# Batch 2's second DFT-47 step ahead of the first tokens, with banks copied into buffers of the turned rows

## The chip, the cores and the metric

The kernel runs on one core of a Trainium2 chip. The metric is the device time of one execution in microseconds (us). The chip's TensorE (PE) multiplies matrices from SBUF into PSUM banks; ScalarE (ACT) and VectorE (DVE) copy, cast and combine; SyncE (SP) and GpSimd (POOL) issue transfers (DMAs) between SBUF and DRAM. The engines run side by side and wait for each other through semaphores.

## The reference

For each of 8 batches of 3008 x 256 values: a real FFT along the sequence, a complex 256 x 256 product with bias, a soft threshold, the inverse FFT; then a feed-forward layer on all 24064 tokens.

```python
X = np.fft.rfft(x, axis=1)
Yr = Xr @ w_r - Xi @ w_i + b_r
Yi = Xr @ w_i + Xi @ w_r + b_i
Yr = np.sign(Yr) * np.maximum(np.abs(Yr) - lam, 0.0)   # Yi likewise
y = np.fft.irfft(Y, n=x.shape[1], axis=1)
h = y.reshape(B * S, D) @ w_in
out = (h * (1.0 / (1.0 + np.exp(-1.702 * h)))) @ w_out
```

## The kernel before, in words

3008 is 64 x 47, so the FFT is done as DFT-47 and DFT-64 products. For each batch, eight DFT-47 steps (`dft47`, L495) take 48 x 512 pieces of x, fill two PSUM banks by four products, copy the banks to SBUF (`dft47_out`, L507, on ACT here) and store them in a DRAM buffer `s1`, one per batch. Later stages (`spectral`, L515) read `s1`, mix, invert, and store to `s2`, from which the tokens come. Each 512 tokens then run through the feed-forward layer in eight parts (`Ffn.up`, `Ffn.down`).

Batch 0 has its own start-up (`first_batch`, L369) in a pool `su` of SBUF, with no trip through `s1`. In it, `rows` (three buffers of 2 KB per partition) hold the turned rows of the first DFT, and `xp` (five pairs, L478) hold pieces of x. Beside batch 0's stages, PE does batch 1's eight DFT-47 steps (`early(n)`, L867) and then one of batch 2 (`do_early(0)`, L938). Their evictions go to `buf2` (L139), seven buffers of one tag that many tiles share.

The change lies where batch 0 ends. Its last inverse step (`stage_inv(5)`) is evicted and stored to `s2`, once by POOL and once by SP (L469). The last third of the first two token pieces can be loaded only then (`load_first`, L605, on SP). While PE waits for it, it runs ten unread products `wm` (L941). Then the pool `su` closes (L948), the pool `ff` opens on the same SBUF, and the first tokens are made (`first_tokens`, L615): products in a bank, a cast to `th` on ACT, the rest `tl` on DVE (`split`, L148). With these the first `Ffn.up` (L694) begins. During the first eight parts, the other steps of batch 2 (`do_early(n)`, n from 1 to 7) and the rounding of further weights (`weights`) run beside it.

Each engine runs its instructions in order. The order on each is set by a scheduler that simulates the program when it is built; `after(...)` holds an instruction behind a named one. SP's transfers take eight completion semaphores (DMAHW0 to DMAHW7) in turn, so each waits for the one eight before it; POOL's use DMASW0 to DMASW7. A tile that takes over SBUF of an earlier one waits until that one's readers are done.

Of the kernel before, what the change touches and what calls it, by code (L numbers as in the profile page):

```python
# [9 lines left out]
F32 = mybir.dt.float32  # L10
# [10 lines left out]
D, DFF = 256, 2048  # L21
# [95 lines left out]
def fourier_mix_then_gated_ffn(ctx: ExitStack, tc: tile.TileContext, x, w_r, w_i, b_r, b_i, w_in, w_out, pack, kbs, out):  # L117
    nc = tc.nc
# [8 lines left out]
    ps_o = ctx.enter_context(tc.tile_pool(name="ps_o", bufs=1, space=PSUM))  # L127
    ps_a = ctx.enter_context(tc.tile_pool(name="ps_a", bufs=4, space=PSUM))
    held = ExitStack()
    su = held.enter_context(tc.tile_pool(name="su", bufs=1))  # L130
    ff = None

    def bank():
        return ps_a.tile([128, 512], F32, name="pa", tag="pa")

    def buf(shape, dt, name, tag=None, bufs=2):
        return wk.tile(shape, dt, name=name, tag=tag or name, bufs=bufs)

    def buf2(name):  # L139
        return buf([128, 2, D], F32, name, tag="w2", bufs=W2)  # L140

    def after(*keys):
        held = ExitStack()
        for k in keys:
            held.enter_context(tc.issue_after(done_at[k]))
        return held
# [5 lines left out]
    last = [None]  # L152

    def mm(ps, w, t, start=True, stop=True):
        last[0] = nc.tensor.matmul(ps, lhsT=w, rhs=t, start=start, stop=stop).ins  # L155
# [9 lines left out]
    def const(shape, dt, name):  # L165
        return cst.tile(shape, dt, name=name, tag=name.rstrip("_"))
# [10 lines left out]
    parts, done_at = {}, {}  # L177
# [41 lines left out]
    def packs_in():  # L219
        pk = ff.tile([128, PKR], F32, name="pk", tag="gt", bufs=1)  # L220
        nc.sync.dma_start(pk, packs)
        return pk

    def rounded_parts(pk):
        parts["i"] = const([128, 2, 2, 128], F32R, "ki_")
        parts["f"] = const([128, NS], F32, "fg_")
        nc.scalar.copy(parts["i"].rearrange("p h z n -> p (h z n)"), pk[:, 0:512])
        nc.scalar.copy(parts["f"], pk[:, 512:536])
        wr, wi = buf2("wr"), buf2("wi")
        for t, w in ((wr, w_r), (wi, w_i)):  # L230
            nc.sync.dma_start(t, w.rearrange("(c p) e -> p c e", p=128))
        parts["h"] = const([128, 3, 2, D], F32R, "wf_h")
        parts["l"] = const([128, 3, 2, D], F32R, "wf_")
        split(parts["h"][:, 2], parts["l"][:, 2], wr)
        for i, op in ((0, ALU.add), (1, ALU.subtract)):
            t = buf2("wd")
            nc.vector.scalar_tensor_tensor(t, wr, -1.0, wi, ALU.mult, op)
            split(parts["h"][:, i], parts["l"][:, i], t)
# [4 lines left out]
    room = [cst.tile([128, NQ // 2 * 896], F32, name=f"room{i}", tag=f"wo_{i}") for i in range(2)]  # L243
# [78 lines left out]
    def weights(n):  # L322
        (down_weights if n % 2 else up_weights)(n // 2)
        if n >= 9:
            load_weights(n + 3)
        elif n in (4, 5):
            load_weights(n + 2)
# [25 lines left out]
    def quarters():  # L353
        return tc.manual_schedule(engines={mybir.EngineType.PE})
# [123 lines left out]
    def xpair():  # L478
        return su.tile([128, 1024], F32, name="xp", tag="xp", bufs=5)

    def xload(b, n, *ts):

        w = 1024 // len(ts)
        for k, t in enumerate(ts):
            for p in range(2):
                at = 1024 * n + w * k
                nc.sync.dma_start(t[64 * p:64 * p + 48], x[b].rearrange("(n p) c -> p n c", p=2)[p, :, at:at + w])
        return [t[:, at:at + 512] for t in ts for at in range(0, w, 512)]
# [3 lines left out]
    def new_s1(b):  # L492
        s1s[b] = dr.tile([2, 64, 2, 8, 2, D], F32, name="s1")

    def dft47(b, n, t, first=None, other=None):  # L495

        ps = [bank(), bank() if other is None else other]
        with quarters():
            if first:
                first(ps[0])  # L500
            dft47_products(ps, t)
        dft47_out(b, n, ps)

    def dft47_products(ps, t):
        for c, p in ((1, 1), (0, 0), (0, 1), (1, 0)):
            mm(ps[p][64 * c:64 * c + 64], kp[64 * p:64 * p + 48], t[c][64 * p:64 * p + 48])

    def dft47_out(b, n, ps, first=nc.scalar.copy):
        s1w = s1s[b].rearrange("c f p n j d -> (c f) p n (j d)")
        for p in range(2):  # L510
            ev = buf2("aev").rearrange("p j d -> p (j d)")
            (nc.scalar.copy if p else first)(ev, ps[p])  # L512
            nc.sync.dma_start(s1w[:, p, n], ev)

    def spectral(b, s2):  # L515
        s1r, s2w = dram_views(s1s[b], s2)
# [83 lines left out]
    def load_first(u, r0, r1, queue):  # L600

        if u not in us:
            us[u] = buf([128, 4, D], F32, "ur", tag="sx", bufs=3) if u else const([128, 4, D], F32, "wf_h")
        s2w = s2s[0].rearrange("c p j d -> (c p) j d")
        done_at["u"] = queue.dma_start(us[u][r0:r1], s2w[r0:r1, 4 * u:4 * u + 4]).ins  # L605
# [32 lines left out]
    def tokens(u):  # L638
# [20 lines left out]
        if step:  # L659
            dft47_out(b, n, p47, nc.vector.tensor_copy)  # L660
# [163 lines left out]
    def new_s2(b):  # L824
        s2s[b] = dr.tile([48, 2, NJ, D], F32, name="s2")
        return s2s[b]
# [3 lines left out]
    def tokens_to(n):  # L830
        nonlocal done
        while done < NB * NU and JP * done < n:
            load_u(done)
            load_x(done)
            if done < 2:
                load_u(done + 1)
            tokens(done)
            done += 1
        load_u(done)
        load_x(done)  # L840
# [22 lines left out]
    x1 = []  # L863
    EARLY = 4
    BLOCKS = (0, 1, 2, 4, 5, 7, 8, 10)

    def early(n):  # L867
        with after(("m", 3 + 2 * n) if n < EARLY else ("m", 11) if n == EARLY else ("i", 5)):
            dft47(1, n, x1[n], claim_now if n < EARLY else None)
        done_at["x", n] = last[0]  # L870

    for n in range(14):
# [29 lines left out]
        if n == 11:  # L902
            early(3)
# [9 lines left out]
        if n == 12:  # L913
            with after(("m", 11), ("t", 11), ("s", 11)):
                i0(4)
                early(EARLY)
# [2 lines left out]
                i0(5)  # L919
    for u in range(2):  # L920
        load_first(u, 64, 96, nc.sync)
    for n in range(EARLY + 1, 8):
        with after("u", ("e", 5)):
            early(n)
    xr = {}

    def load_early(n):
        if n < 8:
            ts = [buf2("xr") if n % 2 else buf([128, 2, D], F32, "xr", tag="co") for c in range(2)]
            xr[n] = xload(2, n, *(t.rearrange("p j d -> p (j d)") for t in ts))  # L930

    def do_early(n):
        load_early(n + 1)
        dft47(2, n, xr.pop(n), claim, ps_o.tile([128, 512], F32, name="po3", tag="po3"))

    load_early(0)
    with after(("x", 7), "u"):
        do_early(0)  # L938
    done_at["x", 8] = last[0]
    for n in range(2):  # L940
        wm = ps_o.tile([128, 512], F32, name="wm", tag=f"po{n}")  # L941
        for i in range(5):
            with after(("x", 8)):
                mm(wm, wi_h[:, 0, 0:128], wi_h[:, 0, 0:512])
    with after(("e", 5), ("v", 11)):
        weights(8)
# [7 lines left out]
    queue, nextb, behind = [], 1, None  # L954
    for n in range(NT * NQ):
        k, q = divmod(n, NQ)
        if q == 0:
            cur = Ffn(k)
        if n != 2:
            with after("down") if q == 1 and k > 1 else ExitStack():  # L960
                cur.up(q)
        if n < NQ:
            if n < 7:
                with after("h", "l"):
                    weights(9 + n)
            if n == 1:
                cur.up(2)
            if n:
                do_early(n)
            if n == 6:  # L970
                with after("h", "l"):
                    rounded_parts(pk)
                ahead = spectral(1, new_s2(1))
                ahead.pop(0)[1]()
            if n == 3:
                pk = packs_in()
        elif not queue and nextb < NB and (nextb < 3 or done >= NU * (nextb - 1)):
            queue = ahead if nextb == 1 else spectral(nextb, new_s2(nextb))
            total, spent, n0 = sum(c for c, _ in queue), 0.0, n
            n1 = NQ * S * nextb // TOK - 16  # L980
            nextb += 1
        while queue and spent < total * (n + 1 - n0) / (n1 - n0):
            c, step = queue.pop(0)
            spent += c
            step()
        need = TOK * (1 + (n + 2) / NQ)
        while queue and need + JP > S * (nextb - 1):
            queue.pop(0)[1]()
        if JP * done < need:
            tokens_to(need)  # L990
        if behind is not None:
            with after("up") if q == 1 and k > 1 else ExitStack():
                behind[0].down(behind[1])
        behind = (cur, q)
# [36 lines left out]
```

## Time and profile before

| | us |
|---|---|
| median of 3 runs (2543.94 to 2545.46) | 2544.39 |
| the profiled execution | 2546.47 |
| its span | 2544.7 |
| PE busy in the span | 2523.1 |
| DVE busy | 1959.7 |
| ACT busy | 1609.9 |
| POOL busy | 90.8 |

The profiled execution is one of its own; its span begins with the first instruction, and 1.8 us lie around it. Busy times are those of single engines, which run side by side. PE's granted clock reads 1.00 over nearly all of the span.

### The profile page before, as it was taken

How to read it: one execution, taken by the hardware profiler on the slowest of the kernel's cores; microseconds unless marked ns; L12 is line 12 of the kernel's file. 1: busy time of each engine (PE TensorE's matmuls, PEld its weight loads, DVE VectorE, ACT ScalarE, POOL GpSimd, SP SyncE). 2: the span in 40 equal slices, each digit the busy share in tenths (PEclk: the TensorE clock that was granted, in tenths of full speed). 3: DMA queues.
4: the chain of work that ended last, by engine and by line, in shares of the span. 5: the costliest groups of instructions: out<-in, count | busy, mean ns of one | idle time of the engine just before them, and what ended most of it. 6: DMA issues, size and time to landing. Idle time of an engine off the chain costs nothing.

```text
span 2544.7 us, 49144 instructions
## 1 busy us (share of the span) xinstructions
PE 2523.1 (99%) x19425; PEld 2231.3 (88%) x19425; DVE 1959.7 (77%) x3285; ACT 1609.9 (63%) x2632; POOL 90.8 (4%) x109
## 2 busy tenths in 40 slices
PE   9999999999999999999999999999999999999999
PEld 7779988888898888888888888988889999888888
DVE  6788877777777777777777877778777787777776
ACT  5566666666666666666666666666666666665655
POOL 0000000000000000000000000000000000000000
PEclk9999999999999999999999999999999999999999
DMA  7753332333323323233233233233332232200000
GB/s 215 241 156 89 92 87 84 96 92 96 91 75 98 94 90 96 66 99 104 81 92 90 84 106 88 82 92 95 90 103 57 58 87 58 60 30 22 24 10 17
DMA packets 163749, 221.80 MB, mean 87 GB/s; under 512 B 18288, under 2 KB 120912, under 8 KB 163520
## 3 DMA queue, kind: packets, MB, share of 16 engines
q1 hardware_dynamic: 161904, 212.96, 29.0%
q0 software_dynamic: 1616, 5.70, 0.8%
q8 instruction: 154, 2.52, 0.4%
q14 instruction: 75, 0.61, 0.1%
HBM read 117.40 MB, written 101.19 MB: 86 GB/s over the span
## 4 chain that ended last, share of the span: by engine, by line
PE 92%; DVE 2%; ACT 2%; issue 2%; DMA 1%; SPq 0%; POOL 0%; POOLq 0%; DVEq 0%; ACTq 0%
PE pa L155 57%; PE po L155 35%; DMA room<-in_x 1%; ACT gb L703 0%; ACT ht L149 0%; PE pi L155 0%; DVE gt L736 0%; DVE hb L150 0%; ACT aev L512 0%; DVE lt L709 0%; DVE lt L150 0%; DMA s<-iev 0%; PE pt L404 0%; DVE tl L150 0%; DVE gt L738 0%
## 5 line engine op out<-in xcount | busy, mean ns | idle before, releaser
L703 ACT ACTIVATE gb<-pa 128x512 f32<-128x512 f32 x752 | 446.0, 599 | 363.4 <-PE pa L155 359.1
L150 DVE TENSOR_TENSOR lt<-gt,ht 128x1024 fp32r<-128x1024 f32 x367 | 449.3, 1224 | 238.0 <-ACT ht L149 237.1
L155 PE MATMUL pa<-th,wi_h 128*128 128x512 f32 x1504 | 594.7, 396 | 2.2 <-ACT aev L512 1.7
L155 PE MATMUL pa<-tl,wi_h 128*128 128x512 f32 x1504 | 589.5, 392 | 0.0
L155 PE MATMUL pa<-th,wi_l 128*128 128x512 f32 x1504 | 587.9, 391 | 0.0
L149 ACT CAST ht<-gt 128x1024 fp32r<-128x1024 f32 x367 | 384.8, 1048 | 209.0 <-DVE gt L738 205.6
L736 DVE TENSOR_TENSOR gt<-gb 128x512 f32<-128x512 f32 x367 | 255.8, 697 | 167.4 <-ACT gb L703 159.6
L150 DVE TENSOR_TENSOR hb<-gb,hb 128x768 fp32r<-128x768 f32 x367 | 349.8, 953 | 14.6 <-ACT hb L149 14.4
L155 PEld LDWEIGHTS pa<-th,wi_l 128*128 128x128 f32 x1504 | 282.7, 188 | 58.9
L155 PEld LDWEIGHTS pa<-th,wi_h 128*128 128x128 f32 x1504 | 283.4, 188 | 51.6 <-ACT aev L512 2.7
L155 PEld LDWEIGHTS pa<-tl,wi_h 128*128 128x128 f32 x1504 | 283.4, 188 | 42.4
L149 ACT CAST hb<-gb 128x768 fp32r<-128x768 f32 x367 | 307.3, 837 | 9.7 <-PE po L155 0.5
L155 PE MATMUL po<-hb,wo_0a 128*128 128x256 f32 (+1 forms) x924 | 231.2, 307 | 1.8 <-ACT o L809 1.2
L155 PE MATMUL po<-hb,wo_0b 128*128 128x256 f32 x924 | 230.3, 306 | 0.0
L155 PE MATMUL pa<-wf_h,zz 128*128 128x256 f32 x1008 | 199.5, 282 | 0.0
L155 PE MATMUL po<-ht,wo_0a 128*128 128x256 f32 (+1 forms) x752 | 191.9, 287 | 1.1 <-DVE o L819 0.9
L155 PE MATMUL po<-ht,wo_0b 128*128 128x256 f32 (+1 forms) x752 | 190.7, 287 | 2.2 <-ACT ht L149 2.0
L155 PE MATMUL po<-ht,wo_1a 128*128 128x256 f32 (+1 forms) x752 | 191.9, 285 | 0.0
L155 PE MATMUL po<-ht,wo_1b 128*128 128x256 f32 (+1 forms) x752 | 190.4, 285 | 0.0
L155 PEld LDWEIGHTS po<-hb,wo_0a 128*128 128x128 f32 x924 | 161.4, 189 | 15.0 <-ACT o L809 1.7
L155 PEld LDWEIGHTS po<-hb,wo_0b 128*128 128x128 f32 x924 | 161.0, 189 | 14.2 <-DVE hb L727 0.2
L737 DVE TENSOR_TENSOR gt<-gb,gt 128x256 f32<-128x256 f32 x367 | 161.2, 439 | 6.6
(179 smaller groups left out, 4227.2 us busy)
## 6 DMA issues: line engine op xcount, KB each, us to landing
s<-aev SPq DMA_DIRECT2D x112, 256.0 KB, 3.7
s<-iev SPq DMA_DIRECT2D x95, 256.0 KB, 2.4
ur<-s SPq DMA_DIRECT2D x124, 192.0 KB, 3.6
out<-o SPq DMA_DIRECT2D x93, 256.0 KB, 2.2
br<-s SPq DMA_DIRECT2D x168, 128.0 KB, 2.9
yd<-mv SPq DMA_DIRECT2D x168, 128.0 KB, 2.4
yr<-yd SPq DMA_DIRECT2D x84, 256.0 KB, 3.1
xt<-in_x SPq DMA_DIRECT2D x80, 192.0 KB, 3.6
```

Source lines behind the costliest of these rows:

```text
L149: nc.scalar.copy(hi, src)
L150: return nc.vector.tensor_tensor(lo, src, hi.bitcast(F32), ALU.subtract)
L155: last[0] = nc.tensor.matmul(ps, lhsT=w, rhs=t, start=start, stop=stop).ins
L703: done_at["g"] = nc.scalar.activation(o, ps.rearrange("p (h n) -> p h n", h=2), AF.Gelu_apprx_sigmoid).ins
L736: nc.vector.tensor_tensor(gt[:, 0:2], b12, gb[:, 0:3:2], ALU.subtract)
L737: nc.vector.tensor_tensor(gt[:, 2], gb[:, 2], gt[:, 0], ALU.subtract)
```

## The change

Step 1 of batch 2 is done ahead of the first tokens, behind step 0; its x goes to a pair of `xp`, loaded earlier. Six unread products are left of ten. The banks of the last two steps of batch 1 and one of batch 2's step 0 are copied to `spare`: three `rows` buffers and two halves of another `xp` pair, in place of `buf2`. The stores of batch 2's two steps are issued on POOL in place of SP. Loads of batch 2's pieces are issued one step sooner in the text.

```diff
-    def dft47_out(b, n, ps, first=nc.scalar.copy):
+    def dft47_out(b, n, ps, first=nc.scalar.copy, room=None, queue=nc.sync):
         s1w = s1s[b].rearrange("c f p n j d -> (c f) p n (j d)")
         for p in range(2):
-            ev = buf2("aev").rearrange("p j d -> p (j d)")
+            ev = room.pop(0) if room else buf2("aev").rearrange("p j d -> p (j d)")
             (nc.scalar.copy if p else first)(ev, ps[p])
-            nc.sync.dma_start(s1w[:, p, n], ev)
+            queue.dma_start(s1w[:, p, n], ev)
...
+    def load_early(n, *ts):
+        if n < 8:
+            ts = ts or [buf2("xr") if n % 2 else buf([128, 2, D], F32, "xr", tag="co") for c in range(2)]
...
-    def do_early(n):
-        load_early(n + 1)
-        dft47(2, n, xr.pop(n), claim, ps_o.tile([128, 512], F32, name="po3", tag="po3"))
+    def do_early(n, po=3, **to):
+        if n:
+            load_early(n + 1)
+        dft47(2, n, xr.pop(n), claim, ps_o.tile([128, 512], F32, name=f"po{po}", tag=f"po{po}"), **to)
+
+    load_early(0)
+    load_early(1, xpair())
+    spare = [su.tile([128, 512], F32, name="rows", tag="rows", bufs=3) for n in range(3)]
+    t = xpair()
+    spare += [t[:, 0:512], t[:, 512:1024]]
     for n in range(EARLY + 1, 8):
         with after("u", ("e", 5)):
-            early(n)
...
-    load_early(0)
+            early(n, room=spare if n > EARLY + 1 else None)
     with after(("x", 7), "u"):
-        do_early(0)
+        do_early(0, room=spare, queue=nc.gpsimd)
     done_at["x", 8] = last[0]
+    with after(("x", 8)):
+        do_early(1, 2, queue=nc.gpsimd)
+    done_at["x", 9] = last[0]
     for n in range(2):
         wm = ps_o.tile([128, 512], F32, name="wm", tag=f"po{n}")
-        for i in range(5):
-            with after(("x", 8)):
+        for i in range(3):
+            with after(("x", 9)):
                 mm(wm, wi_h[:, 0, 0:128], wi_h[:, 0, 0:512])
...
-            if n:
+            if n > 1:
                 do_early(n)
```

What this does to the order shows at three places.

ACT, from the evictions of batch 1's last step to the first casts of the tokens, before (aev: a `buf2` buffer; pa, po: banks; what stands in brackets are the semaphores waited for):

```order
L512 COPY aev_1025<-pa_1016 128x512 [waits DVE_49,PE_49]
L512 COPY aev_1028<-pa_1017 128x512 [waits DMAHW6_49,Activation_49]
L512 COPY aev_1053<-pa_1044 128x512 [waits PE_sequencer_49,DMAHW2_49,PE_49,Activation_49]
L512 COPY aev_1056<-po3_1043 128x512 [waits DMAHW3_49,Activation_49]
L149 CAST th_1097<-pa_1092 128x376 [waits PE_49]
L149 CAST th_1097<-pa_1101 128x376 [waits PE_49]
L149 CAST th_1097<-pa_1111 128x136 [waits PE_49]
```

The same place in the changed kernel, from the eviction of step 6's first bank:

```order
L512 COPY rows_995<-pa_1014 128x512 [waits PE_49]
L512 COPY rows_996<-pa_1015 128x512
L512 COPY xp_998<-pa_1028 128x512 [waits PE_49]
L512 COPY rows_997<-pa_1027 128x512 [waits PE_49]
L512 COPY aev_1052<-po3_1040 128x512 [waits DMAHW6_49,PE_49,Activation_49]
L512 COPY xp_998<-pa_1041 128x512 [waits PE_sequencer_49,PE_49]
L512 COPY aev_1071<-pa_1062 128x512 [waits PE_sequencer_49,DMAHW7_49,PE_49,Activation_49]
L512 COPY aev_1074<-po2_1061 128x512 [waits DVE_49]
L149 CAST th_1111<-pa_1106 128x376 [waits DMAHW2_49,DMAHW6_49,PE_49,Activation_49]
L149 CAST th_1111<-pa_1115 128x376 [waits PE_49]
```

Five evictions go to rows and xp buffers and wait for no transfer; of the same five before, four waited for one (two of them ahead of the rows shown); two more evictions stand ahead of the casts; and the first cast, which waited for PE alone, now waits for two transfers of SP, on DMAHW2 and DMAHW6.

SP's queue from the last store of batch 0 to batch 1's last stores, before (s1_101 is batch 1's `s1`; a store that waits for a DMAHW semaphore takes that one itself):

```order
L469 DMA s2_96<-iev_981 128x2x256 [waits DMAHW6_49,Activation_49]
L605 DMA wf_h_905<-s2_96 32x1024 [waits DMAHW6_49,DMAHW3_49,DMAHW7_49,DMAHW2_49,DMASW7_49]
L605 DMA ur_907<-s2_96 32x1024 [waits DMAHW0_49,DMASW1_49]
L513 DMA s1_101<-aev_995 128x512 [waits DMAHW1_49,Activation_49]
L513 DMA s1_101<-aev_998 128x512 [waits Activation_49]
L513 DMA s1_101<-aev_1010 128x512 [waits Activation_49]
L513 DMA s1_101<-aev_1013 128x512 [waits DMAHW4_49,Activation_49]
L613 DMA ur_1108<-s2_96 48x1024 [waits DMAHW5_49]
L487 DMA xr_1037<-in_x 48x512 [waits DVE_49]
L513 DMA s1_101<-aev_1025 128x512 [waits DMAHW7_49,Activation_49]
L513 DMA s1_101<-aev_1028 128x512 [waits DMAHW0_49,Activation_49]
```

The changed kernel, from the first of the loads L605:

```order
L605 DMA wf_h_905<-s2_96 32x1024 [waits DMAHW4_49,DMAHW1_49,DMAHW5_49,DMAHW0_49,DMASW7_49]
L605 DMA ur_907<-s2_96 32x1024 [waits DMAHW2_49,DMASW1_49]
L513 DMA s1_101<-aev_1008 128x512 [waits DMAHW3_49,Activation_49]
L513 DMA s1_101<-aev_1011 128x512 [waits Activation_49]
L513 DMA s1_101<-rows_995 128x512 [waits Activation_49]
L513 DMA s1_101<-rows_996 128x512 [waits DMAHW6_49,Activation_49]
L613 DMA ur_1122<-s2_96 48x1024 [waits DMAHW7_49]
L613 DMA ur_1122<-s2_96 48x1024
L513 DMA s1_101<-xp_998 128x512 [waits DMAHW1_49,Activation_49]
L513 DMA s1_101<-rows_997 128x512 [waits DMAHW2_49,Activation_49]
```

Two loads of the third token piece (L613) stand together ahead of step 7's stores, and the store of rows_996 takes DMAHW6, that of rows_997 DMAHW2.

POOL's queue behind its store of batch 0, before:

```order
L469 DMA s2_96<-iev_978 128x2x256
L266 DMA wf_h_1131<-in_w_in 128x2x256
L266 DMA wraw_1167<-in_w_in 128x2x256
```

and in the changed kernel:

```order
L469 DMA s2_96<-iev_978 128x2x256
L513 DMA s1_102<-aev_1052 128x512
L513 DMA s1_102<-xp_998 128x512
L513 DMA s1_102<-aev_1071 128x512
L513 DMA s1_102<-aev_1074 128x512
L266 DMA wf_h_1145<-in_w_in 128x2x256
L266 DMA wraw_1181<-in_w_in 128x2x256
```

Four stores of batch 2 (s1_102) stand ahead of two loads of weights.

## Rows read from the trace of the kernel before

**Rows 1.** The page: busy time of each engine.

```profile
PE 2523.1 (99%) x19425; PEld 2231.3 (88%) x19425; DVE 1959.7 (77%) x3285; ACT 1609.9 (63%) x2632; POOL 90.8 (4%) x109
```

**Rows 2.** Busy time by stage: length, then each engine's; TensorE clock, DMA share, GB/s.

```profile
106.00:200.00 94.00, 91.73 (x611) 72.34 (x612) 76.19 (x136) 59.52 (x100) 2.84 (x4) 1.00 0.58 172
200.00:2500.00 2300.00, 2291.34 (x17922) 2045.33 (x17921) 1778.04 (x2952) 1470.27 (x2387) 79.72 (x90) 1.00 0.28 79
```

**Rows 3.** Chain of waits, 94 to 106.5 us: start, length, what.

```profile
95.18 4.38 DMA s<-iev
...
99.57 0.32 SPq L605
...
101.35 3.01 DMA s<-aev
```

**Rows 4.** Timeline of ACT, 94 to 107 us: start, length, instruction, idle before and releaser.

```profile
96.04 1.54 ACT L512 COPY aev<-pa 128x512 f32<-128x512 f32 x3
...
103.76 0.58 ACT L512 COPY aev<-pa 128x512 f32<-128x512 f32 x1 [3.76 <-DMA s<-aev]
...
104.92 1.03 ACT L149 CAST th<-pa 128x376 fp32r<-128x376 f32 x3
```

**Rows 5.** Timeline of PE, 96 to 131 us.

```profile
99.02 2.58 PE L155 MATMUL wm<-wi_h 128*128 128x512 f32 x10
...
106.13 0.87 PE L155 MATMUL pa<-th,wi_h 128*128 128x512 f32 x2 [0.19 <-DVE tl L150]
...
119.45 0.62 PE L155 MATMUL po<-xr,kp 48*64 48x512 f32 x1
...
120.34 0.99 PE L155 MATMUL pa<-kz,ur 48*64 48x47 f32 x52
...
129.75 0.61 PE L155 MATMUL po<-xr,kp 48*64 48x512 f32 x1 [0.71 <-ACT gb L703]
```

**Rows 6.** Busy time in short stretches, columns as in rows 2: DMA share and GB/s last.

```profile
86.00:88.00 2.00, 2.00 (x14) 1.50 (x14) 1.97 (x6) 1.43 (x3) 0.67 (x1) 1.00 0.26 70
...
98.00:100.00 2.00, 2.00 (x15) 1.02 (x10) 2.00 (x5) 1.56 (x3) 0.00 (x0) 1.00 0.04 14
...
100.50:101.00 0.50, 0.50 (x4) 0.40 (x3) 0.06 (x1) 0.00 (x0) 0.00 (x0) 1.00 0.81 197
```

**Rows 7.** Timeline of SP's queue, 99.5 to 112 us: start, time to issue, transfer.

```profile
102.33 0.56 SPq L613 DMA_DIRECT2D ur<-s  x1
...
104.16 0.90 SPq L513 DMA_DIRECT2D s<-aev  x2
...
109.35 1.23 SPq L513 DMA_DIRECT2D s<-aev  x2
```

**Rows 8.** Timeline of POOL, 80 to 125 us.

```profile
104.45 0.72 POOL L266 DMA_DIRECT2D wf_h<-in_w_in  x1 [8.54 <-PE pa L155]
```

**Rows 9.** DMA in 99.5:104, 104:105, 106:112 us: KB each, median us to landing; queues.

```profile
s<-aev SPq DMA_DIRECT2D x4, 256.0 KB, 2.9
...
s<-aev SPq DMA_DIRECT2D x2, 256.0 KB, 5.3
...
q0 software_dynamic: 230, 0.87, 50.2%
q1 hardware_dynamic: 490, 0.91, 50.1%
...
s<-aev SPq DMA_DIRECT2D x2, 256.0 KB, 7.3
```

**Rows 10.** Kernel's end, short stretches as in rows 2; PE's groups by shape, 0 to 30 us.

```profile
2538.50:2539.00 0.50, 0.16 (x2) 0.00 (x0) 0.45 (x2) 0.00 (x0) 0.00 (x0) 1.00 0.00 0
...
2541.50:2542.00 0.50, 0.00 (x0) 0.00 (x0) 0.00 (x0) 0.00 (x0) 0.09 (x1) 0.50 0.17 57
...
L155 PE MATMUL pa<-ka,xp 96*128 96x128 f32 x80 | 9.5, 282 | 0.0
...
L155 PE MATMUL wm<-idle 128*128 128x512 f32 x6 | 5.5, 1088 | 2.3 <-ACT idle L182 2.3
```

More of the change, by code (lines that the diff above doesn't have):

```diff
@@ L493, in new_s1, with dft47 @@
         s1s[b] = dr.tile([2, 64, 2, 8, 2, D], F32, name="s1")
-    def dft47(b, n, t, first=None, other=None):
+    def dft47(b, n, t, first=None, other=None, **to):
         ps = [bank(), bank() if other is None else other]
@@ L501, in dft47 @@
             dft47_products(ps, t)
-        dft47_out(b, n, ps)
+        dft47_out(b, n, ps, **to)
     def dft47_products(ps, t):
@@ L865, in fourier_mix_then_gated_ffn, with early @@
     BLOCKS = (0, 1, 2, 4, 5, 7, 8, 10)
-    def early(n):
+    def early(n, **to):
         with after(("m", 3 + 2 * n) if n < EARLY else ("m", 11) if n == EARLY else ("i", 5)):
-            dft47(1, n, x1[n], claim_now if n < EARLY else None)
+            dft47(1, n, x1[n], claim_now if n < EARLY else None, **to)
         done_at["x", n] = last[0]
@@ L921, in fourier_mix_then_gated_ffn @@
         load_first(u, 64, 96, nc.sync)
+    xr = {}
+    def load_early(n, *ts):
+        if n < 8:
+            ts = ts or [buf2("xr") if n % 2 else buf([128, 2, D], F32, "xr", tag="co") for c in range(2)]
+            xr[n] = xload(2, n, *(t if len(ts) == 1 else t.rearrange("p j d -> p (j d)") for t in ts))
+    def do_early(n, po=3, **to):
[7 more added lines that the diff above has]
+    spare += [t[:, 0:512], t[:, 512:1024]]
     for n in range(EARLY + 1, 8):
         with after("u", ("e", 5)):
-            early(n)
[L925 to L930, printed above, removed]
-    def do_early(n):
-        load_early(n + 1)
-        dft47(2, n, xr.pop(n), claim, ps_o.tile([128, 512], F32, name="po3", tag="po3"))
-    load_early(0)
+            early(n, room=spare if n > EARLY + 1 else None)
     with after(("x", 7), "u"):
-        do_early(0)
+        do_early(0, room=spare, queue=nc.gpsimd)
     done_at["x", 8] = last[0]
+    with after(("x", 8)):
+        do_early(1, 2, queue=nc.gpsimd)
+    done_at["x", 9] = last[0]
     for n in range(2):
         wm = ps_o.tile([128, 512], F32, name="wm", tag=f"po{n}")
-        for i in range(5):
-            with after(("x", 8)):
+        for i in range(3):
+            with after(("x", 9)):
                 mm(wm, wi_h[:, 0, 0:128], wi_h[:, 0, 0:512])
```

## The prediction

> **What bounds the kernel now.** I read the page first: TensorE (PE) is busy for 2523.1 us of a span of 2544.7 us, no other engine over 77% [rows 1]. Next the busy time by stage: after the mixing of batch 0 (from 106 us) PE loses 2.3 us up to 200 us and 8.7 us in the 2300 us behind that [rows 2]. So PE's own stream sets the end, and what the change does to PE between about 95 and 130 us reaches the end almost one to one: there is little idle time later in which a delay could vanish. Third, the chain of waits there [rows 3]: the last store of batch 0's inverse step, issued by POOL, lands 4.38 us later, at 99.56; only then does SP issue the loads of the first tokens (L605), and behind these, held back by the same wait, the stores of early steps. Then comes a store of 3.01 us, an eviction that waited for its buffer, the cast th, the difference tl, and PE's first feed-forward product. ACT's own rows say the same [rows 4]: an eviction waits 3.76 us for a store that still reads its buffer, and the casts, behind it in ACT's order, begin at 104.92. PE bridges the wait for the loads with ten unread products, and then waits only 0.19 us for tl, since the token products themselves have just ended [rows 5].
>
> **The change, part by part.** *The unread products.* Four of ten (2.58 us together, 0.26 each) go and four DFT-47 products come in front of the six others; a step occupied PE for 0.9 us (119.45 to 120.34 [rows 5]), so the gap before the token loads is filled as before: 0.
>
> *The step that left the feed-forward part.* Batch 2's step 1 no longer stands at 119.45: **-0.9 us** of PE. Its two evictions leave ACT there too, and in the order of the changed kernel the casts of down weights now stand behind the two activations whose lateness cost PE 0.71 us at 129.75 [rows 5]: **-0.7**.
>
> *Two more loads ahead.* 2 x 192 KB of x are issued on SP near 85 us, after step 3. The DMA engines are free for three quarters of 86 to 88 us [rows 6], and no engine waits for what stands behind them: 0, bounded by some 0.5 us.
>
> *Evictions into rows and a turned-row pair.* They no longer wait for stores, so ACT is done with all ten near 101 us (pace 0.5 us, from 96.04 [rows 4]). Taken alone that would let the casts begin as soon as the token products give them something, and save the 0.19 us.
>
> *What the same buffers make wait.* But the pool of these buffers closes, and the feed-forward's first tile, th, is laid over two of the three "rows" buffers. In the order rows of the section on the change, the first cast now waits for two of SP's semaphores: the ones that the stores of the second and third "rows" buffer take. The last of them is the tenth entry in SP's queue counted from the first L605 load, and that load still goes at 99.57. With SP's pace (0.45 us for a store, 0.56 for a load of 48 rows [rows 7]) it is issued at about 104.4. Ahead of it stand 2 x 128, 4 x 256, 2 x 192 and 256 KB; with itself 2176 KB. Meanwhile POOL, where batch 2's four stores are put, sends 4 x 256 KB from about 100.5, then its weight loads of 512 KB, from 104.45 as now [rows 8].
>
> When does that store land? The trace doesn't show this load, so I bound it. Below: the four stores issued just behind the token loads, with no POOL traffic, took 2.9 us [rows 9]: 107.3. Those issued at 104.16, with a POOL load beside them, took 5.3; those at 109.35 took 7.3 [rows 7, 9], and there the two queues moved 0.87 and 0.91 MB in 6 us, 50% of the DMA time each [rows 9]: 111.7. Above, by bytes: 2176 KB (2.23 MB) at SP's 0.91 MB in 6 us, from 100.5 when data begins to flow [rows 6], is 14.7 us: 115.2. I take **113.0**, about the middle of the last two: more is queued ahead of this store than of those at 109.35, the nearest row, and the byte count ignores that POOL may pause between its loads.
>
> Here the Trainium skill speaks against the change: "DMA: Bandwidth & Descriptors", section "Issuing engines are not separate DMA queues", says that transfers from SP and POOL run on the same 16 engines, and that a second issuing engine saves only sequencer time. The trace agrees: the halves in rows 9. Were the queues independent, the store would land near 107.3 and the sum below would end at +1.7.
>
> The first feed-forward product: th began at 104.92 and the product at 106.13, 1.2 us later [rows 4, 5]. 113.0 + 1.2 = 114.2, against 106.13: **+8.1 us**. On ACT the activations, on DVE the differences and weight steps, all stand behind the cast, so nothing useful is done meanwhile.
>
> *The clock.* PE then stands idle from 106 to 114. At the kernel's end its granted clock fell from 1.00 (2.4 GHz) to 0.50 (1.2 GHz) within 3 us of the last product [rows 10]. The price of a restart is bounded by nothing (it stays up) and by the only restart in the trace, the kernel's first six passes: 0.915 us each (5.5 us in all, 512 columns), where passes of 128 columns right behind took 0.119 (9.5 us by 80), four of which are 0.476 [rows 10]: 6 x 0.44 = 2.6 us lost. (PEclk reads 1.00 there, so the price rests on durations.) I take **+2.0**, near the upper end, the only restart seen. The Trainium skill, "TensorE: Matmul & The Clock Gate", section "HAM oscillation — how this bites in real kernels", tells of the same pattern: a wait for a DMA lets the clock fall, and the next products start at half speed. The end of this trace agrees.
>
> *Later order.* Behind the first tokens the scheduler's order differs in places to the end: the same work, with 8.7 us of idle time at most to win [rows 2], and as much to lose if the pieces fit worse. I take 0, and 1 or 2 us either way.
>
> Sum: -0.9 - 0.7 + 8.1 + 2.0 = **+8.5 us**. The profiled execution took 2546.47 us, 2.1 above the median of the three runs, 2544.39; its terms carry over unchanged: 2544.4 + 8.5 = **2552.9 us**, 0.33% slower. What a measurement of this kernel can tell from no change is about 0.2%, 5.1 us.
>
> **The rivals.** *The store lands soon* (not slower). If each store takes its own 2.9 us whatever POOL does, it lands at 107.3, the first product comes at 108.5, +2.4; less 1.6; and PE idles only 2.5 us, so that the clock may fall or not (0.9): +1.7, 2546.1 us. For it: the DMA engines are all but idle from 98 us to 100 [rows 6], so that no backlog stands at the start. Against it: 5.3 us already for the stores of 104.16, with half of POOL's traffic. It decides from the landing time: below 109.6 the sum stays under 5.1 us with the clock's price, below 111.6 without it. The Trainium skill, "DMA: Bandwidth & Descriptors", section "Anatomy of one DMA — SWDGE (gpsimd) path", fits 2.0 us plus bytes over 436 GB/s, 2.6 us for 256 KB: an estimate that leads here; no row under load shows it.
>
> *The change frees ACT and nothing waits* (faster, by a little). Casts begin as the products come, PE goes on at 105.94: -0.2 - 0.9 - 0.7 = -1.8, 2542.6 us. For it: the eviction's 3.76 us of waiting do go [rows 4]. Against it: it needs the store landed before 105, half a microsecond after its issue. Only together with a lucky later order would it reach -5.1.
>
> *The clock stays up or the restart is short*, with the store as I have it: +6.5, 2550.9 us, still slower; within my case.
>
> **How the numbers follow.** My case 0.62, the early landing 0.30, the free ACT 0.08. Slower by over 0.2%: my case but for its early tail (landing near 110), 0.61. Faster by over 0.2%: 0.03. Within: 0.36. The range: from 2545.0, which keeps most of the early landing, to 2557.0, which takes in a landing at 115.2 with the full price of the clock (10.3 - 1.6 + 2.6 = 11.3: 2555.7) and 1 us for the later order. My case's own range is 2549.5 to 2557.
>
> **What would show it.** Right: the first th cast idle before it, some 10 us, put down to a store from rows; first feed-forward product near 114; the third rows store 7 us or more from issue to landing; a granted clock of 0.50 around 110 to 117; no wait of 0.7 us for gb near 137. Wrong: the cast within 3 us of the last eviction's place now, or POOL's stores not overlapping SP's. If the first product is late but the end is not, the later stage had slack that rows 2 hide.

## The result, and the profile after

The changed kernel takes 2559.4 us (median of 4 runs, 2557.1 to 2562.21) against 2544.41 for the kernel before (4 runs): 15.0 us more, ratio 1.0059 with a 95% interval of 1.0041 to 1.0076. It is slower by 0.59%. The prediction, 2552.9 us and slower, had the sign and the place of the first wait right; the size was too small, and the time lies 2.4 us above its range.

The profiled execution took 2562.21 us, the longest of the four, with a span of 2560.2, 15.5 us over the span before. PE's busy time grew by only 2.9 us; the rest is waiting. The page's row of busy times:

```profile
PE 2526.0 (99%) x19421; PEld 2232.9 (87%) x19421; DVE 1960.0 (77%) x3285; ACT 1611.0 (63%) x2632; POOL 92.6 (4%) x113
```

The chain of waits of the changed kernel, 94 to 128 us (start, length, what). It runs through SP's queue into one store out of a rows buffer, then through the cast and the difference to the first feed-forward product. In the kernel before it ran through a store of 3.01 us [rows 3].

```profile
101.22 0.95 SPq L513
...
102.22 1.28 SPq L613
...
103.54 1.23 SPq L613
...
104.87 1.26 SPq L513
...
106.23 8.25 DMA s<-rows
...
114.63 0.48 ACT th L149
...
115.14 0.56 DVE tl L150
...
115.83 10.45 PE pa L155 x36
```

ACT's timeline says the same: no eviction waits 3.76 us any more, as one did in [rows 4], and the cast behind them now waits 13.77 us.

```profile
114.63 1.02 ACT L149 CAST th<-pa 128x376 fp32r<-128x376 f32 x3 [13.77 <-DMA s<-rows]
```

Busy time in short stretches has its columns as in [rows 2], the granted clock third from the end. PE stands still from 105.2 us, its granted clock falls to 0.50 (1.2 GHz, "half clock" below), and the first products run at that. The same happens a second time, smaller, behind a wait near 173 us.

```profile
106.00:108.00 2.00, 0.00 (x0) 0.00 (x0) 0.00 (x0) 0.00 (x0) 0.26 (x1) 0.61 1.08 270
108.00:116.00 8.00, 0.17 (x1) 0.20 (x1) 0.86 (x2) 1.02 (x3) 0.00 (x0) 0.50 1.02 311
116.00:120.00 4.00, 4.00 (x10) 3.12 (x11) 1.37 (x5) 0.89 (x3) 0.00 (x0) 0.50 0.39 120
120.00:122.00 2.00, 2.00 (x10) 1.64 (x9) 0.00 (x0) 0.68 (x2) 0.00 (x0) 0.97 0.00 0
...
174.00:178.00 4.00, 3.77 (x15) 3.32 (x16) 3.03 (x6) 2.27 (x4) 0.00 (x0) 0.59 0.76 224
```

To find where 15.5 us come from, the same PE instruction is looked up in both timelines; how much later it starts in the changed kernel is its shift. Of the kernel before, beside [rows 5]:

```profile
114.64 0.64 PE L155 MATMUL po<-xr,kp 48*64 48x512 f32 x1
...
161.37 1.11 PE L155 MATMUL pa<-kr,br 128*128 128x128 f32 x8
163.55 1.13 PE L155 MATMUL pa<-kr,br 128*128 128x128 f32 x8 [1.08 <-ACT co L349]
...
166.26 0.28 PE L155 MATMUL pa<-wf_h,zz 128*128 128x256 f32 x1
```

Of the changed kernel:

```profile
126.21 0.64 PE L155 MATMUL po<-xr,kp 48*64 48x512 f32 x1
...
139.64 0.64 PE L155 MATMUL po<-xr,kp 48*64 48x512 f32 x1
...
171.14 1.05 PE L155 MATMUL pa<-kr,br 128*128 128x128 f32 x8
174.23 1.59 PE L155 MATMUL pa<-kr,br 128*128 128x128 f32 x8 [2.03 <-ACT wo_0b L269]
...
178.51 0.28 PE L155 MATMUL pa<-wf_h,zz 128*128 128x256 f32 x1
```

| instruction | before | changed | later by | what is new |
|---|---|---|---|---|
| first feed-forward product | 106.13 | 115.83 | 9.70 | the cast's wait |
| first DFT-47 product in the feed-forward part | 114.64 | 126.21 | 11.57 | half clock, 1.87 |
| the one that waited 0.71 us before | 129.75 | 139.64 | 9.89 | step 1 and its stall gone, -1.68 |
| first product with br | 161.37 | 171.14 | 9.77 | |
| first wf_h product | 166.26 | 178.51 | 12.25 | a longer wait, 0.9, and half clock, 1.6 |
| end of span | 2544.7 | 2560.2 | 15.5 | 3.25 more, the later loss |

Of the last 3.25 us some 1.6 are lost at one place, near 775 us of the kernel before, where PE's products stand in another order, and 0.9 at a second, near 1510 us; the others are spread.

### The profile page after: what moved, and what is told of

Its sections match the earlier page's. It is cut to its first block, busy times and chain, and to the rows that moved or that the text cites. A ratio compares the mean times of both kernels' runs of the same rounds, so it can differ in the third digit from the quotient of the medians.

```text
span 2560.2 us, 49126 instructions
## 1 busy us (share of the span) xinstructions
PE 2526.0 (99%) x19421; PEld 2232.9 (87%) x19421; DVE 1960.0 (77%) x3285; ACT 1611.0 (63%) x2632; POOL 92.6 (4%) x113
## 4 chain that ended last, share of the span: by engine, by line
PE 91%; issue 3%; DVE 2%; ACT 2%; DMA 1%; SPq 0%; POOL 0%; POOLq 0%; ACTq 0%; DVEq 0%
PE pa L155 56%; PE po L155 34%; ACT gb L703 0%; ACT ht L149 0%; PE pi L155 0%; DVE hb L150 0%; DMA s<-rows 0%; DVE gt L736 0%; ACT aev L512 0%; DVE lt L150 0%; PE wm L155 0%; DVE tl L150 0%; PE pt L404 0%; DVE gt L738 0%; DVE gt L737 0%
## 5 line engine op out<-in xcount | busy, mean ns | idle before, releaser
L155 PE MATMUL pa<-th,wi_h 128*128 128x512 f32 x1504 | 595.7, 397 | 12.3 <-DVE tl L150 10.6
```

## The experiments

Each time is a median, compared with the kernel before on the same chip in the same session (medians 2545.4 to 2545.6). Shifts are those of the same PE instruction against the profile before; each comes from one execution.

**Is it the rows buffers or the step?** Each is built alone. First come the rows alone, in the kernel before (load_early(0) also stands a little earlier in the text):

```diff
+    spare = [su.tile([128, 512], F32, name="rows", tag="rows", bufs=3) for n in range(3)]
+    t = xpair()
+    spare += [t[:, 0:512], t[:, 512:1024]]
...
-            early(n)
+            early(n, room=spare if n > EARLY + 1 else None)
...
-        do_early(0)
+        do_early(0, room=spare)
```

> The kernel before (step 1 in its old place, ten unread products, all stores on SP) with the one edit that the banks of batch 1's steps 6 and 7 and one of batch 2's step 0 go to the rows buffers and xp halves. Theory (the rows buffers under the first cast make the wait, not the step): the store of the third rows buffer is again SP's tenth from the loads of the token pieces, issued some 5.6 us after them as in the experiment with all stores on SP, near 105.1, landed 5.9 us later near 111; first product near 112.2 against 106.13, a stretch at half clock, +7 at 120 us, and with the later order (plus or minus 2) 2550 to 2554 us. Rival (the step ahead of the tokens, with its stores and evictions, costs the time): first product within 1 us of 106.1 and 2543.5 to 2547 us.

Measured 2552.96 us, +7.4. The chain of waits of this kernel, 94 to 126 us:

```profile
103.38 6.00 DMA s<-rows
...
109.53 0.48 ACT th L149
...
110.73 5.80 PE pa L155 x14
```

The store was issued at 103.38, not 105.1, and took 6.0 us. The first product is 4.6 us later, with the half clock the shift is 6.8 us at 137 us, and it is 7.1 at the end. PE's order here is that of the kernel before, and only 0.3 us is lost later. So the edit that was to free ACT makes the wait by itself. Now the step alone, without spare but with its stores on POOL and six unread products, as in the changed kernel:

```diff
-    spare = [su.tile([128, 512], F32, name="rows", tag="rows", bufs=3) for n in range(3)]
-    t = xpair()
-    spare += [t[:, 0:512], t[:, 512:1024]]
...
-            early(n, room=spare if n > EARLY + 1 else None)
+            early(n, room=None)
...
-        do_early(0, room=spare, queue=nc.gpsimd)
+        do_early(0, queue=nc.gpsimd)
```

> The changed kernel without spare: step 1 ahead of the tokens, batch 2's stores on POOL, all banks copied to the shared buffers. Theory (without rows under the first cast the wait is short): the last eviction waits for SP's third store behind the loads of the token pieces, which landed at 105.6 in the changed kernel; first cast 106.3, first product 107.5; then step 2's loads are late as in the experiment without rows (its products waited until 115.85, a loss of 2.7 us and a stretch at half clock of 6.8 us), +3.5 at 122 us, and 2549 to 2552 us. Rival (the step itself holds the casts as long as the rows do): first product 113 or later, 2555 to 2560 us.

Measured 2549.08 us, +3.5. PE's timeline, 97 to 130 us:

```profile
105.48 0.86 PE L155 MATMUL pa<-th,wi_h 128*128 128x512 f32 x2 [0.57 <-DVE tl L150]
...
115.70 0.64 PE L155 MATMUL po<-xr,kp 48*64 48x512 f32 x1 [1.64 <-DMA xr<-in_x]
```

The first product even comes 0.65 us sooner than before, better than expected; the wait for step 2's x is there, 1.64 us, but the clock stayed at 1.00. At 158 us this kernel is 0.7 us ahead of the kernel before; it loses 2.6 us behind that, of which 1.6 near 775 us. So the rival is out, and the total lies in the expected range by luck: the 3.5 us expected by 122 us did not come, and the later loss, which the expectation left out, took their place.

**Why so late a store?** Two edits leave PE's and DVE's order exactly that of the changed kernel. One gives the third rows buffer to a bank of step 0, whose store is POOL's second, and xp halves to step 7:

```diff
-    spare += [t[:, 0:512], t[:, 512:1024]]
+    spare[2:2] = [t[:, 0:512], t[:, 512:1024]]
```

> Third rows buffer given to a bank of batch 2's step 0, whose store is POOL's second; step 7's two banks go to the xp halves. The order on PE and DVE stays that of the changed kernel. Theory (the first cast waits for the store's place in SP's queue): in the changed kernel's trace POOL's second store was issued at 100.27 us and landed 4.2 us later, at 104.5, and SP's store of the second rows buffer at 107.5; so the first cast starts near 107.6, the first feed-forward product near 108.8 (115.83 in the changed kernel), PE's clock does not fall there, and the time is 2559.4 - 7.0 - 1.7 to 3.3 for one or both stretches at half clock = 2549 to 2551 us. Rival (the transfers as a whole are late, whichever buffer is waited for): first product at 113 us or later, 2557 to 2561 us.

Measured 2552.0 us, +6.6. The cast began at 107.60 and the first product came at 108.80, as the theory has it to the tenth:

```profile
107.60 1.02 ACT L149 CAST th<-pa 128x376 fp32r<-128x376 f32 x3 [7.33 <-DMA s<-rows]
```

The total is 1 us above the expectation: PE idled 4.19 us, its clock still fell, and the later loss (+2.3 at 137 us to +4.2 at the end) stayed. So the first product follows the last store that reads a rows buffer. The other edit puts batch 2's stores back on SP:

```diff
-        do_early(0, room=spare, queue=nc.gpsimd)
+        do_early(0, room=spare)
...
-        do_early(1, 2, queue=nc.gpsimd)
+        do_early(1, 2)
```

> Batch 2's four stores go back to SP's queue, behind the store of the third rows buffer; nothing else, order on PE, DVE and ACT as in the changed kernel. Theory (place in SP's queue): the store stays SP's tenth from the loads of the token pieces, so it lands between 113 and 115 and the first product stays at 114 to 116 us: 2557 to 2561 us. Rival (POOL's stores, running beside SP's, make SP's issues and transfers slow: the loads of the third token piece took 1.28 us each to issue, against 0.56 before): the store is issued near 104.4 and takes some 5.5 us, as a store did at that time before, first product near 111 us, 2552 to 2554 us.

Measured 2552.85 us, +7.4: the rival holds and the theory as I had put it falls. The store keeps its place as SP's tenth, but is issued 3 us sooner, of which 1.2 because the loads L605 went sooner in this execution, and takes 5.9 us. SP's timeline here (start, time to issue, transfer):

```profile
97.71 0.32 SPq L605 DMA_DIRECT2D wf_h<-s  x1
...
100.86 1.82 SPq L613 DMA_DIRECT2D ur<-s  x2
...
103.28 0.42 SPq L513 DMA_DIRECT2D s<-rows  x1
```

and in the changed kernel:

```profile
98.88 0.32 SPq L605 DMA_DIRECT2D wf_h<-s  x1
...
100.65 1.52 SPq L513 DMA_DIRECT2D s<-rows  x2
102.22 2.55 SPq L613 DMA_DIRECT2D ur<-s  x2
104.87 1.26 SPq L513 DMA_DIRECT2D s<-xp  x1
106.23 0.39 SPq L513 DMA_DIRECT2D s<-rows  x1
```

What the queues moved in 99.5 to 104 us (packets, MB, share of the 16 engines) bears on the reason. With the stores on SP, SP's queue has the engines alone:

```profile
q1 hardware_dynamic: 692, 1.41, 94.8%
```

In the changed kernel POOL's queue takes 0.56 MB of the same stretch:

```profile
q1 hardware_dynamic: 441, 0.90, 59.6%
q0 software_dynamic: 167, 0.56, 32.1%
```

The sum is nearly the same, 1.41 and 1.46 MB. POOL's stores added no bandwidth here; what they moved, SP's queue didn't, and the store that the cast waits for came later. Counted from the first load L605, so that an execution's own start falls out, that store lands after 11.5 us here and 11.0 in the kernel with the rows alone; with POOL's stores beside it takes 15.6 and 15.7 us in two profiles of the changed kernel and 14.0 with ten unread products (both below). ACT's cast here:

```profile
109.31 1.02 ACT L149 CAST th<-pa 128x376 fp32r<-128x376 f32 x3 [8.44 <-DMA s<-rows]
```

**What is next without the rows?** Step 6's banks go to the xp halves, and all others to shared buffers, since the list is then empty:

```diff
-    spare = [su.tile([128, 512], F32, name="rows", tag="rows", bufs=3) for n in range(3)]
     t = xpair()
-    spare += [t[:, 0:512], t[:, 512:1024]]
+    spare = [t[:, 0:512], t[:, 512:1024]]
```

> No rows buffers: step 6's banks go to the two xp halves, the others to the shared buffers; step 1 stays ahead of the tokens. Theory: the casts wait for PE alone; the first product comes near 105.5 us (106.13 before, less the 0.69 by which the loads of the token pieces are issued earlier), no stretch at half clock, and against the kernel before: -0.7, -1.6 for step 1 gone from the feed-forward part and its stall gone, +0.4 and +2 for the later order near 404 and 775 us as in the changed kernel's trace, +0.6 after 1357: 2544.4 + 0.7 = 2545 us (2543 to 2547). Rival (the stall near 172 us and its low clock are of the order of the loads, not of the first stall): they stay, +2.5, 2547 to 2549 us. Rival (evictions to shared buffers hold ACT as before, its last one ending at 105): first product 106 to 107.5, 2545.5 to 2547.

Measured 2550.43 us, +5.0, above all three expectations. The first product came at 104.64, 1.5 us sooner than before, but PE then ran into the next late transfer, step 2's x, and lost its clock behind it:

```profile
115.85 1.11 PE L155 MATMUL po<-xr,kp 48*64 48x512 f32 x1 [2.75 <-DMA xr<-in_x]
```

```profile
116.00:122.00 6.00, 6.00 (x18) 3.52 (x19) 3.83 (x7) 1.59 (x3) 0.37 (x1) 0.50 0.59 180
```

(the first from PE's timeline, the second from the stretches.) Those loads took 8.8 us from issue to landing (median of four); five loads of x at that place took 5.4 in the kernel before. Whether POOL's stores make them late or what SP now issues ahead of them wasn't tested. So the next kernel, also without rows, lets step 2 run one part later:

```diff
-            if n > 1:
-                do_early(n)
+            if n == 3:
+                do_early(2)
+            if n > 2:
+                do_early(n)
```

> As the experiment without rows, and batch 2's step 2 runs in the fourth part, ahead of step 3, in place of the third. Theory (PE's idle 2.75 us at 112.7 there was the wait for step 2's late x, and the clock fell with it): no idle of over 1 us and no half clock through 130 us, shift -1.5 at 106 us still -1.5 to -2.5 at 125, and with 2 to 3 us for the later order 2544 to 2547 us. Rival (the transfers as a whole are behind, and the next load is late in its place, weights or the third token piece): another idle of 2 us or more between 112 and 125, 2548 to 2551 us.

Measured 2546.93 us, +1.3, ratio 1.0005 (0.9996 to 1.0014). PE is busy from 106 to 132 us without a gap, at full clock:

```profile
106.00:132.00 26.00, 26.00 (x176) 19.71 (x179) 21.37 (x45) 14.70 (x26) 1.95 (x3) 1.00 0.67 208
```

The theory holds. This kernel is 2.5 us ahead of the kernel before at 137 us, and 1.8 behind at the end.

**The clock.** The changed kernel gets forty unread products more (the filler), behind the first tokens' products:

```diff
     tokens_to(TOK)
+    for n in range(2):
+        wm = ps_o.tile([128, 512], F32, name="wm", tag=f"po{n}")
+        for i in range(20):
+            mm(wm, wi_h[:, 0, 0:128], wi_h[:, 0, 0:512])
```

> The changed kernel with 40 more unread products behind the first tokens' products, 9.1 us at 0.227 us each, in the idle 10.6 us ahead of the first feed-forward product. Theory (the idle PE lost its clock, which cost 1.7 us there): the granted clock stays 1.00 through 105 to 125 us, the first product stays near 115.8 and the shift against the kernel before at 140 us is +8.1 instead of +9.8; the total also changes with the later order, which the build makes anew: 2554 to 2559 us. Rival (the slow first products wait for something else, their weights or operands): they take 0.43 us each as before, shift +9.8 at 140 us, 2558 to 2561 us.

Measured 2555.39 us, within the expectation. The stretches of this kernel:

```profile
114.00:116.00 2.00, 1.03 (x3) 0.48 (x3) 1.39 (x4) 1.23 (x5) 0.00 (x0) 1.00 0.91 289
116.00:124.00 8.00, 8.00 (x35) 6.44 (x35) 4.38 (x10) 5.73 (x9) 0.00 (x0) 1.00 0.09 23
```

From the first product, at 114.88, to step 2's first, at 124.63, it is 8.98 us, when 0.77 is taken off for three down products that the new order puts ahead. In the changed kernel it is 10.38 us, in the kernel before 8.51. Of the 1.87 us that I put down to the clock the filler gives back 1.40; the other 0.47 isn't explained. The first product came 0.95 us sooner, in step with loads issued 0.92 sooner. The shift is 7.5 us at 137 us and 7.9 at the end, and the clock reads 1.00 near 173 us too, where the second stall is gone.

**A second profile of the changed kernel.**

> The changed kernel itself, profiled a second time. Theory (the second stall, near 172 us, and its stretch at half clock are chance, as none of the first four experiments shows them): the first product again at 115.8 within 0.5 us, a first stretch at half clock again, no second one, and a profiled time 2 to 3 us below the 2562.2 of the first profile; median 2557 to 2560. Rival (they belong to the shift of the loads by some 10 us): the second stretch is there again, profiled time 2561 to 2563.

Median 2559.24 us, profiled 2561.7. The store was issued at 104.94 and took 8.66 us, the first product came at 114.96 (+8.8). My theory on the second stall falls: it is there again, a wait of 1.9 us and a stretch at half clock, with a shift of 9.5 us before and 11.8 behind. Here the profile names the load of br as what ended it:

```profile
PE pa L155 <- DMA br<-s: 1.9, 1, 1.9
```

(from the list of waits: us in total, times, longest.) The kernel before and the other experiments wait 0.7 to 1.7 us there and keep their clock. It is the same load in the first profile, though that names ACT: in both, the product starts 0.14 us after the fourth load of br has landed, which took 3.98 and 3.81 us from issue to landing, against 3.29 in the kernel before and 2.6 to 3.6 in the other experiments. Why this load is slower when all stands 9 to 10 us later isn't settled.

**The later loss.** All seven kernels so far with six unread products ahead of the tokens lost 1.3 to 2 us near 775 us, and most some more elsewhere; the one that kept ten (rows alone) did not. So here is the kernel before with six in place of ten:

```diff
-        for i in range(5):
+        for i in range(3):
```

> The kernel before with six unread products in place of ten, nothing else. The order at their place is the same but for them; behind 400 us some 360 rows of PE's order stand elsewhere, 94 rows from that of the changed kernel. Theory (the four products cost nothing where they stood, but the schedule that the build simulates is another without them, and its later order is the slower one): shift within 0.3 us of zero up to 400 us, a step of +1.7 us near 775 as in every kernel so far with six, some +1 more by the end: 2547.5 to 2549.5 us. Rival (the later loss comes of step 1's move or of the late start): no step at 775, 2544.5 to 2546.5 us.

Measured 2548.23 us, +2.9, ratio 1.0011 (1.0002 to 1.002). Four products that nothing reads, where PE waits for a transfer anyway, are worth 2.9 us. In the profile the shift is -0.5 us at 400 us, a little past the expected 0.3. It rises by 0.5 us up to 700, by 1.0 across 775 (1.7 at its highest, then partly won back) and by 1.1 near 1510, and is 2.4 at the end. PE's timeline before, and then with six:

```profile
776.64 0.39 PE L155 MATMUL pa<-th,wi_l 128*128 128x512 f32 x1
776.86 0.52 PE L155 MATMUL pa<-yh,ki__1633 128*128 128x256 f32 x3
777.22 0.28 PE L155 MATMUL po<-ht,wo_0a 128*128 128x256 f32 x1
```

```profile
774.53 0.40 PE L155 MATMUL pa<-th,wi_h 128*128 128x512 f32 x1
775.92 0.39 PE L155 MATMUL po<-ht,wo_0a 128*128 128x256 f32 x1 [0.99 <-DVE o L819]
```

With six, down products stand ahead of five up products and three of yh that come first in the kernel before, and wait for DVE to have read their bank (L819). In the lists of waits that group holds 0.9 us once before, and 2.5 us in three waits with six unread products:

```profile
PE po L155 <- DVE o L819: 2.5, 3, 1.0
```

The reverse is the changed kernel with ten, range(5) in place of range(3):

> The changed kernel with ten unread products in place of six, nothing else; PE's later order then differs from that of before in some 50 rows, none of them near 775 us. Theory (the later order of the six is slower by some 3 us): first product near 115.8 and a stretch at half clock as in the changed kernel, +12.3 at 200 us, no step at 775, some +12.5 at the end: 2555 to 2557.5 us. Rival (the later loss follows the late start): +1.7 at 775 and 2558 to 2561 us.

Measured 2555.34 us, 3.9 below the changed kernel of the session before, as expected. Its profile shows no step at 775 us: the shift is +5.7 us at 158 and +5.6 at the end. The expected shift of 12.3 us at 200 us is missed, it is 5.4: that execution was the shortest of five, 2552.26 us, its first product came at 112.44 already, and the second stall is a wait of 0.9 us at full clock. So the profile shows that the later loss goes with the four products back, but not how the 3.9 us of the medians divide.

**The best of it.** This kernel has no rows, step 2 later, and ten unread products:

> The kernel without rows buffers and with batch 2's step 2 in the fourth part, with ten unread products in place of six. Theory: its shift of -1.4 us at 164 us stays to the end, less 0.3 as in the kernel with the rows edit alone: 1 us below the kernel before, 2543.5 to 2545.5 us. Rival (its step near 775 is its own): as with six, 2546 to 2548 us.

Measured 2544.45 us, -0.9, ratio 0.9998 (0.9989 to 1.0007): below the changed kernel by some 15 us, but not to be told from the kernel before. In the profile the gain at 137 us, 2.1, is still 1.9 at the end.

## Why the prediction was wrong, point by point

*The unread products: 0.* **Failed.** Leaving four out cost nothing at their own place. But the build's simulated schedule has them too, and without them orders the work behind otherwise: +2.9 us (the kernel before with six). *Later order: 0, 1 or 2 us either way* failed with it: 3.25 us in the profile. I had seen that the order differs to the end and had not asked which line of the edit makes it differ.

*The step that left: -0.9 and -0.7.* Right: the shift of 11.57 falls to 9.89, -1.68.

*The evictions free ACT.* Right: the last ends at 100.9. *Two more loads: 0.* No run has them alone; the kernel with the step alone holds them, and is not late where the tokens begin.

*Which wait ends last.* Right: the cast waits for the third rows buffer's store, the tenth of SP's queue, and the rows alone make the kernel slower.

*When that store lands: 113.0.* **Mis-sized**: 114.5, and 113.6 in the second profile. Its 8.25 us (8.66) are about the 8.6 that 113.0 less 104.4 gave. What failed is the start: I had SP issue at the pace of [rows 7], so that 4.8 us would pass from the first load L605 to this store, when 7.35 passed (7.06 in the second profile). The two loads of 48 rows took 2.55 us and not 1.1, and the three stores ahead on rows and xp 2.78 and not 1.35. The issue was 1.8 us later than I had it, although the loads ahead went 0.7 sooner. The first product is later by 9.70 instead of 8.1. The Trainium skill's "DMA: Bandwidth & Descriptors", section "Issuing engines are not separate DMA queues", holds here: with the stores on either queue nearly the same bytes moved, 1.41 and 1.46 MB. The fit from the same page's section "Anatomy of one DMA — SWDGE (gpsimd) path", an estimate of 2.6 us for 256 KB, does not hold under this load: POOL's own stores took 4.7 us (median of three) and 4.2.

*The clock: +2.0.* Right: 1.87, of which the filler gave back 1.40. **Missing** from the sum is the second stall near 173 us: 0.9 of waiting and 1.6 of half clock. I had counted one wait and one restart; why the loads of br come later there stays open.

So +8.5 became +15.5 in the profile by 1.6 for the landing, 2.5 for the second stall and 3.25 for the later order, less some 0.3 of small differences. The range had 4.1 us of room above the forecast, and the three add up to 7.35. By medians the parts alone are 7.4 (rows) and 3.5 (step, with POOL's stores and six unread products). Their sum, 10.9, is below the 13.6 to 15.0 of both together, so the parts don't add: only together do POOL's stores delay the store that the cast waits for. With these back on SP the changed kernel is 7.4 us over the kernel before in place of 13.6. In the profiles the first product then comes 4.4 to 5.3 us sooner than in the changed kernel, and the second stall, 2.3 to 2.5 us, is gone too.

## What to carry to other kernels

A buffer that an eviction may have "for free" can lie under the next stage's first tile; look up which transfer must leave it, and where that stands in its queue, before counting what the eviction saves. Here a second issuing engine lent no bandwidth: with its stores beside, the one store that mattered landed 14.0 to 15.7 us after the first load in place of 11.0 to 11.5. Where a build simulates a schedule, an instruction that costs nothing at its place can still set the order of everything behind; compare the orders with that line alone taken out.

## What the runs showed of the hardware that was not expected

SP took longer to issue its transfers when POOL's stores ran beside. From the first load L605 to the issue of the third rows buffer's store, SP's tenth transfer, 5.0 us (rows alone, with two smaller loads among the ten) and 5.6 (stores back on SP) passed without them, and 6.2 (ten unread products), 7.06 and 7.35 (changed kernel) and 7.6 (filler) with them. Single transfers vary more: the two loads of 48 rows took 1.82 us with the stores back on SP, and 2.55 and 1.55 in the two profiles of the changed kernel. Why SP takes longer isn't shown.

PE's granted clock fell to half behind idle times of 1.88 and 2.03 us (changed kernel, near 173 us), 2.75 (no rows) and 4.19 (third rows buffer on POOL). It stayed at 1.00 behind 1.48 us (filler), 1.64 (step alone) and 1.68 (no rows, step 2 later). I had only looked for it behind the long one.
